# Retention and two feed-forward layers on one core: the lead of the displaced weight slots goes from 16 to 8 elements

## The chip, the cores and the metric

The kernel runs on one core of a Trainium2 chip. The metric is the device time of one execution in microseconds, the median of several runs.

## The reference

Attention with a decay instead of a softmax (retention), over 4 batches, 8 heads, 576 positions and 64 channels, gives 2304 tokens of 512 channels. Two feed-forward layers of 512 x 2048 x 512 follow, with different activations:

```python
ret = scores * Dmat[None, :, :, :]          # scores = scale * q k^T, Dmat = gamma**(i-j), lower triangle
attn_out = np.matmul(ret, v)                # -> x [2304, 512]
...
h = x @ w_in;  g = np.maximum(0.01 * h, h);  x = g @ w_out        # first layer
...
h = x @ w_in;  g = h - np.tanh(h);           out = g @ w_out      # second layer
```

## The kernel before

**Number format.** In the layers every operand is split into a high and a low part (fp32r), and every product is made of three matmuls: high by high, high by low, low by high. A matmul has a weight load of 128 x 128 of its own (128 columns of 4 bytes are 512 bytes in each partition) and then moves 512 or 256 columns (2048 or 1024 bytes in each partition).

**Stages.** `retention()` computes the retention chunk by chunk in fp32. Between its pieces it places 12 units of the first layer: `unit_h` (L782) multiplies 256 tokens by two blocks of `w_in` (matmuls of L789, 24 in a unit), `unit_o` (L802) multiplies the result by `w_out` (L814, 24 in a unit). All of these move 256 columns. `layers()` then goes through the list `steps`: a step is one block of 128 hidden channels by 512 or 256 tokens.

- First layer (`m == 0`): `h_mm` (L275) moves the activations `xh` and `xl`; `o_mm` (L428) moves the hidden activations `g`, with `w_out` as weights. 2304 tokens are blocks of 512 and a remainder of 256; in the first group some more of 256 went to the units of the retention stage.
- Second layer (`m == 1`): blocks of 512 tokens are "folded": one level of a Strassen-like scheme, in `h_folded` (L309), moves 256 columns of `xh`, `xl` or of the prepared combinations `xe`. `o_mm` (L428) moves 512 columns of `w_out`, with `g` as weights. In one folded pair of steps, pieces of L309 (6 to 18 matmuls) and of L428 (6 matmuls) alternate. The remainder of 256 tokens goes through `h_mm` with 256 columns.

The order of the work is written out by hand; no scheduler changes it.

**Addresses.** `xh`, `xl` and the store `w` of all weight and `g` slots lie one behind the other in one pool, and their sizes are multiples of 512 bytes. `xe` stands at the other end of the memory, behind a pad of 320 bytes. In the built program `xh`, `xl`, `xe` and `w` all begin at 160 bytes modulo 512. A slot in `w` is 4096 bytes, and a slot that is asked for with `lead` begins `LEAD` elements further on:

```python
    def slot(k, lead):                                              # L81
        at = k * 1024 + (LEAD if lead else 0)
    def w_place(m, g, j):                                           # L85
        return slot(N_OUT + N_G + (4 + j if m == 0 else j), m or g == 0)
    def w_out_place(m): ...  return slot((turn["o"] - 1) % N_OUT, m)       # L90
    def g_place(m): ...      return slot(N_OUT + (turn["g"] - 1) % N_G, m) # L94
    def g_at(s):                                                    # L343
        at = LEAD if m == 0 and n < 512 else 0
```

So the lead applies to `w_in` of the first group of the first layer and of the whole second layer, to `w_out` and `g` of the second layer, to `g` of the first layer where 256 columns move, and to `g` of the units in the retention stage. With `LEAD = 16` the distance "start of the moving operand minus start of the weights", modulo 512 bytes (called the gap below), is:

| matmuls | columns | count | gap |
|---|---|---|---|
| L309, second layer | 256 | 1344 | 448 (that is -64) |
| L275, second layer and first group of the first | 256 | 240 | 448 |
| L789, units | 256 | 288 | 448 |
| L814, units | 256 | 288 | 64 |
| L428, first layer | 256 | 192 | 64 |
| L275, first layer, first group | 512 | 48 | 448 |
| L275, first layer, other groups | 256 | 144 | 0 |
| L275, first layer, other groups | 512 | 576 | 0 |
| L428, first layer | 512 | 624 | 0 |
| L428, second layer (both operands with lead) | 512 | 864 | 0 |

Of the kernel before, what the change touches and what calls it, by code (L numbers as in the profile page):

```python
# [20 lines left out]

LEAD = 16

TANH_T = 0.5
RHO_C = 0.0020447001866573740
# [8 lines left out]
def retention_moe_moe(  # L36
# [41 lines left out]
    N_OUT, N_G, N_IN = GF, 3, 8  # L78
    wide_all = keep.tile([P, (N_OUT + N_G + N_IN) * 1024 + LEAD], F32R, name="w")

    def slot(k, lead):  # L81
        at = k * 1024 + (LEAD if lead else 0)
        return wide_all[:, at:at + 1024].rearrange("p (i c) -> p i c", i=2)
# [259 lines left out]
    def g_at(s):  # L343
        m, g, t0, n, f = steps[s]
        at = LEAD if m == 0 and n < 512 else 0
        return slice(at, at + n)
# [810 lines left out]
```

## Time and profile before

| | |
|---|---|
| median of 3 runs | 859.57 us (859.44 to 859.59) |
| the profiled execution | 860.67 us |
| its span, first to last instruction | 858.6 us |
| TensorE matmuls, busy | 844.0 us (98%) |
| TensorE weight loads, busy | 748.7 us (87%) |
| VectorE, ScalarE, GpSimd, busy | 605.7, 446.0, 376.0 us |

The profiled execution's own time is 2.07 us over its span and 1.10 us over the median. Matmuls are pipelined: the duration that a row gives to one is longer than the distance from its start to the start of the next. What a matmul costs in a row of equal ones is therefore read from starts: the start of the first row behind them, less their own start, divided by their count.

### The profile page before, as it was taken

To read this page: it belongs to the slowest core of one execution; us is meant where nothing else is said; L and a number is where in the kernel's file an instruction comes from. 1 tells how busy PE (TensorE), PEld (TensorE's weight loads), DVE (VectorE), ACT (ScalarE), POOL (GpSimd) and SP (SyncE) were. 2 spreads that over 40 slices of the span, in tenths; PEclk is the share of its full clock that TensorE was granted. 3 is DMA by queue.
4 is the path that set the end of the run, shared out by engine and by line. 5 is a ranking of instruction groups with operands and counts; after the bars stand their busy time and mean duration, and the time that the engine had idled before them with its cause. 6 is when DMAs were issued, how large, how long until landed. Compare 5 with 4: busy or idle time off the path is not lost.

```text
span 858.6 us, 15267 instructions
## 1 busy us (share of the span) xinstructions
PE 844.0 (98%) x5750; PEld 748.7 (87%) x5750; DVE 605.7 (71%) x1050; ACT 446.0 (52%) x877; POOL 376.0 (44%) x304
## 2 busy tenths in 40 slices
PE   6999999999999999999999999999999999999997
PEld 5899999888988888888888899888999899999996
DVE  5996876687685777658764687756766677677765
ACT  3553444453345334453544577765566566566663
POOL 2542231140046203364365387745445445544553
PEclk9999999999999999999999999999999999999999
DMA  9945754323455433645454512491225311563112
GB/s 326 327 134 182 232 191 168 127 100 131 138 199 211 155 122 101 243 172 150 169 188 155 196 56 94 158 357 73 75 98 203 141 74 74 207 234 123 50 50 74
DMA packets 38793, 134.42 MB, mean 157 GB/s; under 512 B 4416, under 2 KB 5952, under 8 KB 36672
## 3 DMA queue, kind: packets, MB, share of 16 engines
q1 hardware_dynamic: 38288, 133.25, 43.6%
q8 instruction: 45, 0.74, 0.3%
q10 hardware_dynamic: 432, 0.20, 0.1%
q14 instruction: 28, 0.23, 0.1%
HBM read 97.26 MB, written 36.18 MB: 155 GB/s over the span
## 4 chain that ended last, share of the span: by engine, by line
PE 92%; DVE 5%; issue 1%; DMA 1%; ACT 0%; POOL 0%; SPq 0%; DVEq 0%
PE a L428 41%; PE h L275 22%; PE h L309 18%; PE a L814 3%; PE x_b L789 3%; PE o L739 1%; PE sc L647 1%; PE o L728 1%; DVE cw L183 1%; DVE pt L670 1%; PE x_c L696 1%; DMA kv<-in_vn 1%; DVE xl L748 0%; DVE st L706 0%; DVE cw L172 0%
## 5 line engine op out<-in xcount | busy, mean ns | idle before, releaser
L428 PE MATMUL a<-w 128*128 128x512 f32 (+1 forms) x1680 | 394.3, 377 | 0.0
L428 PEld LDWEIGHTS a<-w 128*128 128x128 f32 x1680 | 293.4, 188 | 47.5
L256 POOL TENSOR_TENSOR w<-cw,w 128x512 fp32r<-128x512 f32 x80 | 113.4, 1433 | 230.8 <-ACT w L255 211.6
L275 PE MATMUL h<-xh,w 128*128 128x512 f32 (+1 forms) x672 | 187.0, 349 | 0.0
L368 POOL TENSOR_TENSOR v<-t,u 128x512 f32<-128x512 f32 (+1 forms) x76 | 93.5, 1230 | 97.8 <-ACT t L365 93.7
L275 PEld LDWEIGHTS h<-xh,w 128*128 128x128 f32 x672 | 119.4, 188 | 17.0
L400 POOL TENSOR_TENSOR w<-v,w 128x512 fp32r<-128x512 f32 (+1 forms) x76 | 95.9, 1262 | 62.9 <-ACT w L399 62.9
L354 ACT ACTIVATE w<-h 128x512 fp32r<-128x512 f32 (+1 forms) x68 | 37.2, 547 | 159.7 <-PE h L275 115.5
L275 PE MATMUL h<-xl,w 128*128 128x512 f32 (+1 forms) x336 | 117.0, 348 | 0.0
L309 PE MATMUL h<-xh,w 128*128 128x256 f32 x512 | 100.9, 281 | 0.1
L309 PEld LDWEIGHTS h<-xe,w 128*128 128x128 f32 x576 | 80.9, 189 | 9.5 <-DVE mk L303 1.8
L183 DVE SCALAR_TENSOR_TENSOR cw<-st,cw 128x512 uint32<-128x512 uint32 x96 | 86.5, 901 | 2.5
L394 DVE SCALAR_TENSOR_TENSOR v<-q,v 128x512 f32<-128x512 f32 (+1 forms) x76 | 61.9, 814 | 36.0 <-POOL v L368 36.0
L309 PEld LDWEIGHTS h<-xh,w 128*128 128x128 f32 x512 | 83.1, 190 | 2.7 <-DVE v L397 1.4
L309 PE MATMUL h<-xe,w 128*128 128x256 f32 x576 | 84.1, 282 | 0.4 <-DVE mk L303 0.4
L513 DVE TENSOR_TENSOR acc<-a,acc 128x512 f32<-128x512 f32 (+1 forms) x113 | 71.3, 657 | 17.0 <-PE a L428 17.0
L364 ACT ACTIVATE u<-h 128x512 f32<-128x512 f32 (+1 forms) x80 | 44.2, 553 | 73.3 <-DVE h L303 51.5
L399 ACT ACTIVATE w<-v 128x512 fp32r<-128x512 f32 (+1 forms) x76 | 45.3, 596 | 62.6 <-DVE v L397 60.1
L172 DVE TENSOR_SCALAR cw<-cw 128x512 f32<-128x512 f32 x64 | 35.1, 548 | 57.6 <-ACT cw L166 57.3
L309 PE MATMUL h<-xl,w 128*128 128x256 f32 x256 | 71.8, 281 | 0.0
L275 PEld LDWEIGHTS h<-xl,w 128*128 128x128 f32 x336 | 63.3, 188 | 8.6
L383 DVE TENSOR_TENSOR h<-h,t 128x512 f32<-128x512 f32 (+1 forms) x80 | 51.4, 642 | 14.8 <-ACT t L365 14.7
(89 smaller groups left out, 1161.7 us busy)
## 6 DMA issues: line engine op xcount, KB each, us to landing
kept<-w SPq DMA_DIRECT2D x48, 512.0 KB, 3.2
w<-kept SPq DMA_DIRECT2D x48, 512.0 KB, 4.8
xe<-xkept SPq DMA_DIRECT2D x12, 1536.0 KB, 6.4
st<-in_w2i SPq DMA_DIRECT2D x16, 512.0 KB, 3.5
st<-in_w1i SPq DMA_DIRECT2D x12, 512.0 KB, 4.3
st<-in_w1o SPq DMA_DIRECT2D x12, 512.0 KB, 3.5
xkept<-xe SPq DMA_DIRECT2D x4, 1536.0 KB, 10.5
kv<-in_vn SPq DMA_DIRECT2D x16, 320.0 KB, 4.9
```

The lines of the kernel that those rows point to most:

```text
L183: nc.vector.scalar_tensor_tensor(out=t["w"], in0=t[src], scalar=scalar, in1=t["w"], op0=op, op1=ALU.bitwise_or)
L256: nc.gpsimd.tensor_tensor(out=wp[:, 1, :], in0=wf, in1=wp[:, 0, :].bitcast(F32), op=ALU.subtract)
L275: nc.tensor.matmul(out=ps[:, :n], lhsT=w[:, wi, cs], rhs=x[:, kk, t0:t0 + n], start=kk == 0 and i == 0, stop=kk == KK - 1 and i == 2,)
L309: nc.tensor.matmul(out=out_, lhsT=w[:, wi_, at:at + P], rhs=x(xi, kk), start=start and kk == 0 and j == 0, stop=stop and kk == 1 and j == ...
L364: nc.scalar.activation(out=u[:, :n], in_=h, func=AF.Square)
L368: nc.gpsimd.tensor_tensor(out=v[:, :n], in0=t_[:, :n], in1=u[:, :n], op=ALU.mult)
L383: nc.vector.tensor_tensor(out=h, in0=h, in1=tmp[s][1][:, :n], op=ALU.subtract)
L394: nc.vector.scalar_tensor_tensor(out=v, in0=q, scalar=RHO_A, in1=v, op0=ALU.add, op1=ALU.mult)
L399: nc.scalar.activation(out=gt[:, 0, g_at(s)], in_=v, func=AF.Copy)
L400: (nc.gpsimd if m else nc.vector).tensor_tensor(out=gt[:, 1, g_at(s)], in0=v, in1=gt[:, 0, g_at(s)].bitcast(F32), op=ALU.subtract)
L428: nc.tensor.matmul(out=o, lhsT=l, rhs=r, start=f == 0 and i == 0 and d % pack == 0, stop=f == GF - 1 and i == 2 and (d + 1) % pack == 0, s ...
L513: nc.vector.tensor_tensor(out=dst, in0=a, in1=dst, op=ALU.add)
```

## The change

One constant becomes 8. Leads of 64 bytes become leads of 32 bytes: a gap of 448 becomes 480 (that is -32), a gap of 64 becomes 32, and a gap of 0 stays, since there both operands move or neither does. `w` gets 32 bytes shorter, so what is placed behind it (the tiles of the retention stage, two tiles of the second layer's activation) moves by 32 bytes as well. No instruction is added, removed or moved on any engine.

```diff
-LEAD = 16
+LEAD = 8
```

## Rows read from the trace of the kernel before

**Rows 1.** The page: span, busy time and share of TensorE, clock, chain by engine
```profile
span 858.6 us, 15267 instructions
PE 844.0 (98%) x5750; PEld 748.7 (87%) x5750; DVE 605.7 (71%) x1050; ACT 446.0 (52%) x877; POOL 376.0 (44%) x304
PEclk9999999999999999999999999999999999999999
PE 92%; DVE 5%; issue 1%; DMA 1%; ACT 0%; POOL 0%; SPq 0%; DVEq 0%
```

**Rows 2.** Busy time by stretch: retention, first layer, second layer
```profile
core 0: us, PE busy (x) PEld busy (x) DVE busy (x) ACT busy (x) POOL busy (x), PEclk, DMA share, GB/s
0.00:144.00 144.00, 134.64 (x1705) 125.79 (x1706) 111.49 (x239) 64.97 (x150) 47.66 (x52) 1.00 0.66 222
144.00:469.00 325.00, 325.00 (x1623) 276.45 (x1622) 226.69 (x368) 142.86 (x277) 115.41 (x82) 1.00 0.46 160
469.00:858.60 389.60, 384.35 (x2426) 346.49 (x2424) 267.54 (x443) 238.21 (x451) 212.95 (x172) 1.00 0.35 130
```

**Rows 3.** Groups by line and shape, TensorE: count, busy us, mean ns, idle before
```profile
L309 PE MATMUL h<-xh,w 128*128 128x256 f32 x512 | 100.9, 281 | 0.1
L309 PE MATMUL h<-xe,w 128*128 128x256 f32 x576 | 84.1, 282 | 0.4 <-DVE mk L303 0.4
L309 PE MATMUL h<-xl,w 128*128 128x256 f32 x256 | 71.8, 281 | 0.0
...
L428 PE MATMUL a<-w 128*128 128x256 f32 x192 | 25.2, 280 | 0.0
```

**Rows 4.** Timeline, TensorE, second layer: start, us, line, operands, count
```profile
662.17 2.88 PE L428 MATMUL a<-w 128*128 128x512 f32 x12
664.89 0.28 PE L275 MATMUL h<-xh,w 128*128 128x256 f32 x1
...
666.30 2.88 PE L428 MATMUL a<-w 128*128 128x512 f32 x12
669.02 0.28 PE L275 MATMUL h<-xh,w 128*128 128x256 f32 x1
```

**Rows 5.** Timeline, TensorE, first layer, gap 0 with 256 columns
```profile
217.50 0.40 PE L275 MATMUL h<-xh,w 128*128 128x256 f32 x2
217.74 0.28 PE L275 MATMUL h<-xl,w 128*128 128x256 f32 x1
217.85 0.40 PE L275 MATMUL h<-xh,w 128*128 128x256 f32 x2
218.09 0.28 PE L275 MATMUL h<-xl,w 128*128 128x256 f32 x1
218.22 0.28 PE L275 MATMUL h<-xh,w 128*128 128x256 f32 x1
218.34 2.91 PE L428 MATMUL a<-w 128*128 128x512 f32 x12
221.08 0.28 PE L275 MATMUL h<-xh,w 128*128 128x256 f32 x1
...
222.51 2.91 PE L428 MATMUL a<-w 128*128 128x512 f32 x12
225.26 0.28 PE L275 MATMUL h<-xh,w 128*128 128x256 f32 x1
```

**Rows 6.** Chain of waits, longest pieces in order of time: start, us, line, count
```profile
145.73 4.09 PE h L275 x36
...
154.02 2.80 PE h L275 x12
...
231.13 2.76 PE h L275 x12
...
477.70 2.83 PE h L275 x24
```

**Rows 7.** Chain of waits, pieces in order of time, one unit in the retention stage
```profile
81.91 2.72 PE a L814 x24
...
88.47 2.94 PE x_b L789 x24
```

**Rows 8.** Timeline, TensorE, second layer, at two short waits of TensorE
```profile
487.32 0.97 PE L309 MATMUL h<-xe,w 128*128 128x256 f32 x6
488.13 0.86 PE L428 MATMUL a<-w 128*128 128x512 f32 x3
488.83 0.96 PE L309 MATMUL h<-xe,w 128*128 128x256 f32 x6
```

**Rows 9.** Timeline, TensorE, first layer, first group: where the quicker spacing ends
```profile
149.66 1.53 PE L428 MATMUL a<-w 128*128 128x256 f32 x12
151.02 0.28 PE L275 MATMUL h<-xh,w 128*128 128x256 f32 x1
...
152.44 1.58 PE L428 MATMUL a<-w 128*128 128x256 f32 x12
```

## The prediction

> **What bounds the kernel now.** I read the page first. TensorE is busy for 98% of the span and makes 92% of the chain of waits, and its clock was granted in full in every slice [rows 1]. The stretches say the same with more detail: from 144 us on TensorE idles only 5.25 us in all, and 9.4 us in the retention stage before, while VectorE, the next busiest engine, works 605.7 of 858.6 us [rows 1, 2]. So the time is the number of matmuls times their spacing, and a nanosecond more or less per matmul arrives at the end almost undiminished. Durations do not tell the spacing: they are 281 or 282 ns for 256 columns in all groups [rows 3]. I therefore took starts from the timeline and lengths of unbroken pieces from the chain, and put beside each the gap that the code gives (moving operand minus weights, modulo 512 bytes).
>
> **What the gap does today.** With 512 columns and a gap of 0, twelve matmuls take 662.17 to 664.89, or 226.7 ns each [rows 4]; with a gap of 448 twelve take 2.80 us, or 233.3 ns [rows 6]. With 256 columns and a gap of 0, seven take 217.50 to 218.34, or 120.0 ns each [rows 5]; with a gap of 448 in the second layer 24 take 2.83 us, or 117.9 ns [rows 6]. The same gap of 448 has a second, quicker spacing: 36 matmuls at 145.73 take 4.09 us, or 113.6 ns [rows 6], and 24 of L814 at a gap of 64 take 2.72 us, or 113.3 ns [rows 7]. At 151.02 the quick spacing ends: twelve of L428 before it go at 113.3 ns, and twelve of L275 behind it, at the old gap, at 118.3 ns [rows 9]. So a spacing depends on the gap and also on how the stream was entered. Lastly the way out counts. Twelve matmuls of 512 columns behind a block at gap 448 take 666.30 to 669.02, 2.72 us, as anywhere [rows 4]. Behind a block at gap 0 they take 2.74 and 2.75 us [rows 5], some 25 ns more, and behind one at gap 64 they take 2.76 us [rows 6], 40 ns more. Today's gap thus has a way out that costs nothing, and it is taken 142 times in the second layer (I counted the places on the timeline where a row of L428 with 512 columns stands behind one of L309 or L275).
>
> **The change part by part.** Nothing is added, removed or reordered; only spacings can move. No trace shows a gap of 480 or of 32 in these matmuls, so each term is bounded by the nearest gaps, 0 on one side and 448 or 64 on the other. 480 lies in the middle between 448 and 512, which is 0, and 32 between 0 and 64, and I take the middle of the prices too.
>
> Term A, 256 columns in the two layers: 512 + 576 + 256 = 1344 of L309 [rows 3], 240 of L275 (48 in the first group, 192 in the second layer, by the code) and 192 of L428 [rows 3], together 1776. From 117.9 ns to the middle between 117.9 and 120.0, which is 118.95: +1.05 x 1776 = +1.9 us. Bounds: 120.0 ns gives +2.1 x 1776 = +3.7 us; the quick 113.3 ns gives -4.6 x 1776 = -8.2 us.
>
> Term B, the 142 ways out into 512 columns: from 0 to the middle between 0 and 25 ns, +12.5 x 142 = +1.8 us. Bounds: 0, and 40 ns, which is +5.7 us. Less than nothing is not to be had there, since 2.72 us is what twelve such matmuls take with no disturbance.
>
> Term C, 288 + 288 matmuls of the units in the retention stage, which are at 113.3 ns now [rows 7] (of L789 the 24 from 88.47 take 2.94 us with a wait at their head): the middle between 113.3 and 120.0 is 116.7, +3.35 x 576 = +1.9 us. Bounds: 0, if the quick spacing survives, and +6.7 x 576 = +3.9 us. TensorE is the chain there as well, so this isn't hidden.
>
> Term D, 48 matmuls of 512 columns in the first group: from 233.3 to the middle, 230.0: -3.3 x 48 = -0.2 us, between -0.3 and 0.
>
> Term E, what moves without a change of its gap: 864 matmuls of L428 in the second layer, whose two operands both move by 32 bytes. Those of the first layer, without the lead, and these, 64 bytes further on, have one spacing today, 226.7 ns ([rows 4] for these; the rows of twelve in [rows 5] differ by the way out alone). A move by 64 bytes does nothing, then; one by 32 isn't shown. I take 0 and keep one step between spacings that occur, 233.3 - 226.7 = 6.6 ns, as a bound either way: 5.7 us. The fp32 matmuls of the retention stage, whose tiles move by 32 bytes together, and the operands of VectorE, ScalarE and GpSimd I take at 0: those three have 253 us or more of slack over the span [rows 1]. If that cover were gone, the 5.25 us of idle time in the second layer [rows 2] is where it would show first.
>
> Sum: +1.9 + 1.8 + 1.9 - 0.2 = **+5.4 us**. For the profiled execution, 860.67 us (span 858.6 and 2.07 around it), that is 866.1 us; it stood 1.10 us over the median, so for the median it is 859.57 + 5.4 = **865.0 us**, 0.6% more.
>
> **A rule that speaks against any change.** The rows say that 512 columns cost 226.7 or 233.3 ns with nothing but the place of the weights being different [rows 4, 6]. The Trainium skill, page "TensorE: Matmul & The Clock Gate", section "Step-by-step: what each phase is for", states that the moving operand and the weight load have independent read ports, and that loading the next weights takes no read bandwidth from the running matmul. By that rule every term above is 0 and the time stays at 859.6 us. This trace disagrees with it by those 6.6 ns, so I give it a rival's place, not the forecast.
>
> **The rivals.**
>
> 1. *Like a gap of 0.* 32 bytes may be too little to part the two streams. Then all upper ends hold, with 25 ns for the way out: 3.7 + 3.6 + 3.9 - 0.3 = +10.9 us, 870.5 us. For it: the price at 0 and at 448 differs by only 2.1 ns, so the useful distance may be the whole 64 bytes. Against it: nothing shows a threshold.
>
> 2. *Faster: the quick spacing holds in the second layer.* The 113.3 ns exist at gaps of 448 and 64, so the weights can keep up. The mechanism is the entry: behind 512 columns the stream falls at once into 117.9 ns, and only behind a wait of TensorE does it get quick. If at 480 it enters at 113.3 ns, term A is -8.2 us, and with ways out between 0 and 25 ns (0 to +3.6 us) the time is 851.4 to 855.0, say 853 us. Three matmuls of 512 columns behind such a quick stretch, 488.13 to 488.83, took 0.70 us instead of 0.68 [rows 8], so the way out is probably not free. It decides itself where the average of a block of 12 falls below 117.9 - 25/12 = 115.8 ns; above that, a free way out lost costs more than the spacing gives. Term E at its favourable end would be added.
>
> 3. *No change.* Either the two streams meet in units of 64 bytes or more, so that 32 and 64 bytes count alike, or the retention gap and the layers' gap shift against each other to near nothing: 859.6 us, within 1.7.
>
> **How the numbers follow.** This kernel's measurement can tell about 0.2%, 1.7 us, from no change. The forecast, something between the neighbours, has 0.34 (861.5 to 868 us); rival 1 has 0.14 (868 to 872); rival 2 has 0.32 (851 to 857.8), since an unknown place in a system with two spacings may as well land in the better one; rival 3 has 0.20. Slower is 0.34 + 0.14 = 0.48, the same 0.20, faster 0.32. The range goes from 852 to 871: it holds the forecast, most of rival 1 and 2, and leaves out what term E might add at either end. The likeliest case's own range is 861.5 to 868.
>
> **What would show it.** In the trace of the changed kernel: the spacing of 12 matmuls of L275 between two blocks of L428 in the second layer (now 118; forecast 119, rival 1: 120, rival 2: 113); the twelve of L428 behind them (now 2.72 us; 2.73 forecast, 2.75 by rival 1); 24 of L814 (now 2.72 us; 2.80 forecast, 2.88 by rival 1); and 512 columns in the second layer away from a way out (226.7 ns, if term E is nothing). The forecast is wrong if the 256-column blocks get quicker than 117.9 ns, or if a spacing changes whose gap did not.

## The result, and the profile after

The changed kernel takes **865.18 us** (863.40 to 865.46) beside 859.58 us for the kernel before on the same chip: 5.6 us more between the medians. The ratio, which compares means, is 1.0056 (1.0042 to 1.0069), or 4.8 us. Forecast were 865.0 us, 5.4 us slower. The profiled execution took 865.04 us instead of 860.67, and its span grew by 4.4 us; the accounting below divides up that span.

The page of the changed kernel, the lines that answer to [rows 1]:

```profile
span 863.0 us, 15267 instructions
PE 849.1 (98%) x5750; PEld 752.2 (87%) x5750; DVE 604.5 (70%) x1050; ACT 446.0 (52%) x877; POOL 374.9 (43%) x304
PE 95%; DVE 2%; issue 1%; DMA 1%; POOL 0%; ACT 0%; SPq 0%; DVEq 0%; POOLq 0%
```

The same instructions, the same 98%, and a chain that is TensorE's even more than before. The three stretches of the changed kernel answer to [rows 2]:

```profile
core 0: us, PE busy (x) PEld busy (x) DVE busy (x) ACT busy (x) POOL busy (x), PEclk, DMA share, GB/s
0.00:144.00 144.00, 135.20 (x1694) 126.35 (x1694) 110.75 (x239) 64.09 (x148) 46.54 (x51) 1.00 0.66 221
144.00:469.00 325.00, 325.00 (x1631) 276.88 (x1628) 226.35 (x368) 142.42 (x276) 114.51 (x81) 1.00 0.46 160
469.00:863.00 394.00, 388.93 (x2432) 348.93 (x2431) 267.41 (x445) 239.52 (x454) 213.81 (x172) 1.00 0.35 129
```

The clock is granted in full in all three. TensorE idles 5.07 us in the last stretch (5.25 before), so the added time isn't waiting: TensorE's matmuls stand further apart. In the first 144 us it starts 1694 matmuls where it started 1705; it is behind already when the retention stage ends.

The longest pieces of the chain of waits of the changed kernel (start, us, what) answer to [rows 6, 7]:

```profile
88.92 3.04 PE x_b L789 x24
91.96 2.80 PE a L814 x24
...
147.21 4.26 PE h L275 x36
...
232.74 2.75 PE h L275 x12
...
479.20 2.84 PE h L275 x24
```

24 of L814 went from 2.72 to 2.80 us (116.7 ns each), 36 of L275 in the first group from 4.09 to 4.26 (118.3 ns, where the quicker spacing of 113.6 had been), 24 of L275 in the second layer from 2.83 to 2.84. The way out is read on the timeline of the changed kernel, TensorE, which answers to [rows 4]:

```profile
665.01 2.91 PE L428 MATMUL a<-w 128*128 128x512 f32 x12
667.75 0.28 PE L275 MATMUL h<-xh,w 128*128 128x256 f32 x1
...
669.17 2.91 PE L428 MATMUL a<-w 128*128 128x512 f32 x12
671.92 0.28 PE L275 MATMUL h<-xh,w 128*128 128x256 f32 x1
```

665.01 to 667.75 is 2.74 us and 669.17 to 671.92 is 2.75 us for twelve matmuls of 512 columns, where [rows 4] had 2.72; the twelve of 256 columns between them, 667.75 to 669.17, take 1.42 us, 118.3 ns each.

For the whole kernel I took the distance from each matmul's start to the next start in both traces and summed the differences by group:

| matmuls | gap | change, us | term and forecast |
|---|---|---|---|
| 1344 of L309 | -64 to -32 | +1.04 | A |
| 192 of L275, second layer | -64 to -32 | +0.09 | A |
| 48 of L275, 256 columns, first group | -64 to -32 | +0.16 | A |
| 192 of L428, 256 columns | 64 to 32 | -0.09 | A: together +1.20, forecast +1.9 |
| 888 of L428, 512 columns, behind blocks of the second layer | 0, the way out from -64 to -32 | +1.82 | B: forecast +1.8 |
| 288 of L789 and 288 of L814 | -64 to -32, 64 to 32 | +1.13 and +0.66 | C: +1.79, forecast +1.9 |
| 48 of L275, 512 columns, first group | -64 to -32 | +0.01 | D: forecast -0.2 |
| first layer, gap unchanged | 0 | -0.12 in all | E: forecast 0 |
| fp32 matmuls of the retention | unchanged | -0.45 | E: forecast 0 |

The 888 are the 864 of the second layer and two blocks of twelve of the first, which run between blocks of L275 of the second. The sum is +4.25 us; with a first matmul that starts 0.14 us later that is the span's +4.4.

### The profile page after: what moved, and what is told of

Read it like the earlier page. It is cut to its first block, busy times and chain, and to the rows that moved or that the text cites. A ratio compares the mean times of both kernels' runs of the same rounds, so it can differ in the third digit from the quotient of the medians.

```text
span 863.0 us, 15267 instructions
## 1 busy us (share of the span) xinstructions
PE 849.1 (98%) x5750; PEld 752.2 (87%) x5750; DVE 604.5 (70%) x1050; ACT 446.0 (52%) x877; POOL 374.9 (43%) x304
## 4 chain that ended last, share of the span: by engine, by line
PE 95%; DVE 2%; issue 1%; DMA 1%; POOL 0%; ACT 0%; SPq 0%; DVEq 0%; POOLq 0%
PE a L428 41%; PE h L275 22%; PE h L309 18%; PE a L814 4%; PE x_b L789 4%; PE o L739 2%; PE sc L647 2%; PE o L728 1%; PE x_c L696 1%; DMA kv<-in_vn 1%; PE x_e L660 0%; POOL w L256 0%; DVE cw L183 0%; PE x_e L654 0%; DVE v L394 0%
## 5 line engine op out<-in xcount | busy, mean ns | idle before, releaser
L428 PE MATMUL a<-w 128*128 128x512 f32 (+1 forms) x1680 | 396.3, 378 | 0.0
L428 PEld LDWEIGHTS a<-w 128*128 128x128 f32 x1680 | 293.5, 188 | 49.3
L275 PE MATMUL h<-xh,w 128*128 128x512 f32 (+1 forms) x672 | 187.1, 349 | 0.0
L275 PEld LDWEIGHTS h<-xh,w 128*128 128x128 f32 x672 | 119.5, 188 | 16.9
L275 PE MATMUL h<-xl,w 128*128 128x512 f32 (+1 forms) x336 | 117.3, 349 | 0.0
L309 PE MATMUL h<-xh,w 128*128 128x256 f32 x512 | 101.7, 282 | 0.0
L309 PEld LDWEIGHTS h<-xe,w 128*128 128x128 f32 x576 | 81.0, 188 | 9.4 <-DVE mk L303 1.5
L309 PEld LDWEIGHTS h<-xh,w 128*128 128x128 f32 x512 | 82.9, 188 | 2.6 <-DVE v L397 1.3
L309 PE MATMUL h<-xe,w 128*128 128x256 f32 x576 | 84.3, 282 | 0.3 <-DVE mk L303 0.3
L309 PE MATMUL h<-xl,w 128*128 128x256 f32 x256 | 71.9, 281 | 0.0
L275 PEld LDWEIGHTS h<-xl,w 128*128 128x128 f32 x336 | 63.3, 188 | 8.6
```

The lines of the kernel that those rows point to most:

```text
L275: nc.tensor.matmul(out=ps[:, :n], lhsT=w[:, wi, cs], rhs=x[:, kk, t0:t0 + n], start=kk == 0 and i == 0, stop=kk == KK - 1 and i == 2,)
L309: nc.tensor.matmul(out=out_, lhsT=w[:, wi_, at:at + P], rhs=x(xi, kk), start=start and kk == 0 and j == 0, stop=stop and kk == 1 and j == ...
L428: nc.tensor.matmul(out=o, lhsT=l, rhs=r, start=f == 0 and i == 0 and d % pack == 0, stop=f == GF - 1 and i == 2 and (d + 1) % pack == 0, s ...
```

## Experiments

Each run is timed beside the kernel before on the same chip; "gap" is again moving operand minus weights. "Way out" is the time that a run of 512 columns behind 256 columns takes over 226.7 ns for each of its matmuls, in the median. A "seam" is the place where the number of columns changes; its gap is the last moving operand before it minus the first weights behind it. Sums "by starts" come from the one execution of each run whose trace is kept, "L428 with 512 columns" being the 888 above.

**Does the place count, or the distance?** All operands 32 bytes further on, all gaps as before (lines move by one).

```diff
-        [P, 80], F32, name="edge"
+        [P, 72], F32, name="edge"
+    keep.tile([P, 8], F32, name="pad")
```

> The lead stays at 16, so every gap is as before; all operands (xh, xl, xe, w and the tiles behind them) stand 32 bytes further on, as the displaced slots and the tiles behind w do (in the other direction) in the change. Gap theory (the distance of moving operand and weights sets the spacing): nothing moves, 859.6 us within 0.2%; 117.9 ns for 256 columns and 226.7 ns for 512 in the second layer, no price for the way out. Place theory (the address itself, modulo 64 bytes, sets it): the spacings of the changed kernel or others, 863 us or more, or a gain.

Measured: 860.72 beside 860.80 us, ratio 0.9999 (0.9990 to 1.0009). The chain of waits of this run:

```profile
91.89 2.72 PE a L815 x24
...
661.51 1.41 PE h L276 x12
662.93 2.72 PE a L429 x12
```

2.72, 1.41 and 2.72 us are the figures of the kernel before. A place 32 bytes further on is worth nothing by itself; what is left of the change is the distance.

**The two halves of the change, each alone.** The new lead in the second layer only, and in the units and the first layer only. For both, `slot` takes a number in place of a flag:

```diff
+LEAD_IN, LEAD_OUT = 8, 8
...
-        at = k * 1024 + (LEAD if lead else 0)
+        at = k * 1024 + lead
...
-        return slot(N_OUT + N_G + (4 + j if m == 0 else j), m or g == 0)
+        return slot(N_OUT + N_G + (4 + j if m == 0 else j), LEAD_IN if m else LEAD * (g == 0))
...
-        return slot((turn["o"] - 1) % N_OUT, m)
+        return slot((turn["o"] - 1) % N_OUT, LEAD_OUT * m)
...
-        return slot(N_OUT + (turn["g"] - 1) % N_G, m)
+        return slot(N_OUT + (turn["g"] - 1) % N_G, LEAD_OUT * m)
```

> Lead 8 in the second layer alone (w_in, w_out and g of it), 16 elsewhere. Gap theory: what the two traces differ by in the second layer, L309 +1.0, L275 +0.1, the way out +1.8, together +2.9 us: 862.5 us; 118.3 ns for 256 columns and some 15 ns for each way out. If the second layer's part came from what runs before it (another phase of the stream on entry), nothing: 859.6 us.

Measured: 864.03 us, ratio 1.0038 (1.0026 to 1.0050), +3.2 us. By starts, L309 +1.05 us, L275 +0.10, L428 with 512 columns +1.83; the units unchanged.

The other half has `LEAD = 8` and `LEAD_IN, LEAD_OUT = 16, 16`.

> Lead 8 in the units of the retention stage and in the first layer, 16 in the second layer. w keeps its size, so the tiles of the retention stage stay where they were. Gap theory: L789 +1.1, L814 +0.7, first group +0.2, together +1.9 us: 861.5 us, the fp32 matmuls as before. If the 32 bytes by which the retention tiles moved made that stage's difference: 859.6 us. The parts of this run and of the run with lead 8 in the second layer alone should add up to the whole change.

Measured: 862.29 us, ratio 1.0017 (1.0007 to 1.0026), +1.5 us. By starts, L789 +1.06 us, L814 +0.74, the 48 of L275 with 256 columns +0.17, those with 512 columns 0.00. The second layer keeps its old spacing: the chain of waits of this run shows a unit at 2.80 us and the later block at 2.72.

```profile
90.94 2.80 PE a L815 x24
...
666.97 2.72 PE a L429 x12
```

3.2 and 1.5 us make 4.7 of the 5.6, and the ratios 0.55 of 0.56%; by starts the halves add up to the whole (2.98 + 1.97 beside 4.90 us for the same groups). The two halves don't visibly act on each other.

**No lead, twice the lead, four times the lead.** One constant each: `LEAD = 0`, `LEAD = 32`, `LEAD = 64`.

> Lead 0: every gap is 0. By the rows of before at a gap of 0 (120.0 ns for 256 columns, 25 ns for each way out into 512 columns, 226.7 ns for 512): 1776 x 2.1 = +3.7, 142 x 25 ns = +3.6, 576 x 6.7 = +3.9, the 48 of 512 columns -0.3, together +10.9 us: 870.5 us. If the middle price of the changed kernel is no step between two ends but the price of every small gap: 865 us.

Measured: 869.51 us beside 860.80, ratio 1.0101 (1.0086 to 1.0115), +8.7 us. The chain of waits:

```profile
93.25 2.88 PE a L814 x24
...
663.03 1.44 PE h L275 x12
```

> Lead 32, a gap of 384 (-128) and 128. If the price falls steadily with the distance (120.0 at 0, 118.3 at 32, 117.8 at 64 bytes): 117.5 ns or a little less in the layers, at most -0.5 us, and a way out of unknown price between 0 and 40 ns, up to +5.7 us. If the quick 113.3 ns is what a stream gets that starts far enough from a meeting: -8.0 us before the way out. If both streams meet in any case once in a weight load, whatever the distance: the layers as before, 859.6 us.

Measured: 871.11 us beside 859.28, ratio 1.0134 (1.0118 to 1.0149), +11.8 us: the dearest of all and beyond every figure that was expected, although its two streams are further apart. The chain of waits:

```profile
92.44 2.84 PE a L814 x24
...
663.00 1.44 PE h L275 x12
```

> Lead 64, a gap of 256 in all displaced matmuls, half of the 512 bytes, as far as two streams can be apart. The same three theories as with lead 32: a steady fall, at most -0.5 us before the way out (0 to +5.7 us); the quick spacing, -8.0 us before the way out; no difference, 859.6 us.

Measured: 868.07 us, ratio 1.0103 (1.0084 to 1.0122), +8.8 us. The chain of waits:

```profile
91.37 2.88 PE a L814 x24
...
661.15 1.44 PE h L275 x12
```

A distance of 256 bytes costs what a distance of 0 costs: L309 takes 161.25 us in both kernels, L428 with 512 columns 205.57 and 205.58. So the price repeats after **256 bytes**, not 512, and the gap of 448 in the prediction is -64, that of 480 is -32. The five leads side by side (changes against the kernel before, by starts except for the time; the spacing is the median of the unbroken blocks of 256 columns in the second layer):

| lead | gap of 256 columns | time, us | L309, us | its spacing, ns | way out, ns | L428 with 512, us | units, us |
|---|---|---|---|---|---|---|---|
| 0 | 0 | +8.7 | +2.24 | 119.3 | 27 | +2.98 | +2.96 |
| 8 | -32 | +5.6 | +1.04 | 118.3 | 15 | +1.82 | +1.79 |
| 16 | -64 | 0 | 0 | 117.8 | 0 | 0 | 0 |
| 32 | -128 | +11.8 | +2.84 | 119.8 | 41 | +4.46 | +2.42 |
| 64 | -256 | +8.8 | +2.25 | 119.3 | 27 | +2.98 | as lead 0 |

The 576 matmuls of L275 whose gap stays at 0 serve as a control: with the four other leads their sum moves by less than 0.1 us. Lead 32 has its 256 columns at -128, where 512 columns of L275 cost 232 ns (11.14 us for the 48 of the first group).

**What the way out is made of.** The lead of `w_in` at 16 and of `w_out` and `g` at 8: 256 columns keep -64 and 512 columns keep 0, but at both seams, into 512 columns and back, the operand that still moves stands -32 from the first weights of the next block.

```diff
+LEAD_IN, LEAD_OUT = 16, 8
```

> The other half: in the second layer w_out and g have the lead of 8, w_in keeps 16. The 864 matmuls of 512 columns keep their gap of 0 and move by 32 bytes (term E alone); the 256-column ones stay at 448. Gap theory: 226.7 ns and 117.8 ns as before, 0 for term E; at the seam g loads at a gap of 480. If the way out's price is left behind by the 256-column stream: 0, no change at all. If the gap at the seam makes it: +1.8 us. If the place counts: 226.7 ns becomes 220 or 233 ns, 5.7 us either way.

Measured: 863.17 us beside 859.28, ratio 1.0041 (1.0026 to 1.0056), +3.9 us, more than the 1.8 expected of a seam. L428 with 512 columns costs 4.10 us more, though its own gap is what it was, and L309 1.05 us less. The timeline, TensorE:

```profile
667.46 2.94 PE L429 MATMUL a<-w 128*128 128x512 f32 x12
670.24 0.28 PE L276 MATMUL h<-xh,w 128*128 128x256 f32 x1
```

2.78 us for twelve, 231.7 ns each. So the distance at the seams counts, and it can set the pace of all that follows. By position in the runs of six, before: 227, 227, 227, 227, 227, 232 ns; with the change: 233, 233, 227, 228, 228, 231; here: 231, 235, 231, 234, 228, 238. With the change the first two matmuls pay and the stream finds back; here it doesn't.

The counterpart, `w_in` at 8 and the others at 16, **missed its aim**:

```diff
+LEAD_IN, LEAD_OUT = 8, 16
```

> In the second layer w_in alone has the lead of 8, w_out and g keep 16. The 256-column matmuls run at a gap of 480, the 512-column ones at 0, but at the seam the weights that load under the last 256 columns (g) stand at a gap of 448 to them. If the way out's price is left behind by the 256-column stream: 118.3 ns and some 15 ns for each way out, +2.9 us over before, as with both at 8. If it is the gap at the seam that makes it: 118.3 ns and 0, +1.2 us.

Measured: 900.28 us, ratio 1.0473 (1.0458 to 1.0489). The last `g` slot with a lead of 16 reaches 8 elements into the first `w_in` slot with a lead of 8, so that each overwrites a piece of the other, the second layer computes something else, and the two wait for each other. The waits of TensorE (us in total, times, longest us):

```profile
PE h L310 <- POOL w L401: 18.7, 4, 5.2
...
PE h L276 <- POOL w L401: 4.5, 1, 4.5
```

These waits are new; of the spacing the run says nothing.

**More distances in one run.** Each group of the second layer with a `w_in` lead of its own, and 64 elements of room between the slots:

```diff
+IN_LEADS = (8, 24, 48, 56)
+G_LEAD, OUT_LEAD = 16, 16
```

> In the second layer w_in stands at another lead in each of its four groups: 32, 96, 192 and 224 bytes (gaps of -32, -96, +64 and +32 modulo 256); w_out and g keep 64 bytes, units and first layer keep 64. Each slot of w_in has 256 bytes of room behind it, so that no two slots overlap; half of the slots thereby change their distance from 0 to 256 or from 448 to 192 modulo 512. If the price repeats every 256 bytes: units and first layer as before (117.3 to 118.5 ns in the units, 119.3 and 226.7 ns in the first layer). Group 0 asks the seam question again, stream at -32, weights of g at -64 to it: 118.3 ns in both cases; a way out of 15 ns if the stream leaves it behind, 0 if the seam makes it. For the others: a spacing of 117 to 120 ns by the prices seen so far; the quick 113.3 ns is what would beat both kernels, 1.7 us in each group.

Measured, one execution of each: 864.58 us beside 861.36. Group times are read from starts in the traces, from the first L309 of a group to that of the next (the last one to the same matmul of its last block of L275). The four groups have gaps of -32, -96, +64 and +32 and took 96.41, 95.61, 80.29 and 94.56 us, where before they took 95.37, 94.68, 79.53 and 93.72: each about 1 us more. The way out is 26, 26, 27 and 32 ns, although the seam towards 512 columns is at -64 as before; what changed is the distance of the 256 columns themselves and the seam back, and the run doesn't separate the two. The first group repeats the question of the run with overlapping slots and answers neither 0 nor 15 ns but some 26. Half of the `w_in` slots of the units and the first layer went from a distance of 0 to 256, or from -64 (448) to -64 (192), with no change over 0.15 us: the period again.

In the next, 512 columns are at +64:

```diff
+IN_LEADS = (16, 24, 48, 56)
+G_LEAD, OUT_LEAD = 16, 32
```

> In the second layer w_out at 128 bytes and g at 64, so that the 512-column matmuls run at a gap of +64 instead of 0; w_in at 64, 96, 192 and 224 bytes in groups 0 to 3. If the price of 512 columns has its least value at 0 (233.3 at -64, 232 at -128): 230 ns and more, some 3 us or more over before from 864 matmuls. If the side matters (moving operand ahead of the weights, as at +64 with 256 columns, where 116.9 to 118.1 ns were seen): 220 to 226 ns, up to 5.7 us less than before. Group 0 against before shows what the seams then cost.

Measured, one execution of each: 861.76 us beside 861.36. The third group, with 256 columns at +64, keeps the quick spacing from 689 us to its end at 751, as its chain of waits shows:

```profile
699.72 2.04 PE h L312 x18
701.76 1.39 PE a L431 x6
```

2.04 us is 113.3 ns each; but six of 512 columns take 1.39 us, 231.7 ns. The group takes 79.25 us, 0.28 less than before: what the one block gains the other gives back.

The last scan has everything at +64, +32, -32 and -64 with `w_out` at 256 bytes:

```diff
+IN_LEADS = (48, 56, 72, 80)
+G_LEAD, OUT_LEAD = 48, 64
```

> Second layer with w_out at 256 bytes (0 modulo 256) and g at 192, so 512 columns run at +64; w_in at 192, 224, 288 and 320 bytes in groups 0 to 3, which gives 256-column gaps of +64, +32, -32 and -64; the weights of g stand at +64 to the last 256 columns everywhere. The run before had its quick spacing, 113.5 ns, where all of 256 at +64, 512 at +64 met, but 512 columns then cost 5 ns more each. If a seam whose gap equals that of the stream is free, as at -64 in the kernel before: group 0 gives 113.5 ns and no way out, at least 1.7 us less than before in that group (93.7 us of 95.4). If the way out is the price of having been quick: 113.5 ns and 30 ns per way out, and the group is within 0.5 us of before. Groups 1 to 3 have unequal seams: 116.9 to 118.5 ns and ways out of 25 to 35 ns.

Measured, one execution of each: 860.43 us beside 859.36. The groups take 95.32, 95.52, 80.36 and 92.98 us. The first one, the best hope, is where it was (95.37); the last one is 0.74 us quicker than before (93.72). Its chain of waits, from its beginning:

```profile
751.43 2.09 PE h L312 x18
...
761.77 2.05 PE h L312 x18
763.82 1.37 PE a L431 x6
```

2.05 us for 18 is 113.9 ns, with 1.37 us for six of 512 columns, 228.3 ns: quick 256 columns, and 512 columns only 1.6 ns over their 226.7.

**The candidate.** The distances of that last group in all four:

```diff
+IN_LEAD, G_LEAD = 80, 48
...
-        return slot((turn["o"] - 1) % N_OUT, m)
+        return slot((turn["o"] - 1) % N_OUT, 0)
```

> The last group of the run before, everywhere in the second layer: w_in at 64 bytes (modulo 256), g at 192, w_out at 0, so that 256 columns run at a gap of -64, 512 columns at +64, and the weights of g stand at +64 to the last 256 columns. That group took 92.98 us where the kernel before takes 93.72. If the gaps alone set the price, also in the other groups: 114.4 ns for 256 columns, 15 ns for a way out, and -0.74 x 4 = -3.0 us, 856.6 us. If it was the phase in which the stream arrived in that one group: 859.6 us or more, with 117.8 ns again.

Measured: 863.26 us (861.79 to 864.35) beside 859.70, ratio 1.0035 (1.0022 to 1.0047): slower, where 856.6 was expected. The groups take 95.23, 95.58, 80.83 and 95.38 us. With the same addresses the stream has **two paces**. The chain of waits, where one turns into the other:

```profile
603.64 2.05 PE h L310 x18
605.69 1.37 PE a L429 x6
...
611.88 0.75 PE h L310 x6
612.63 1.40 PE a L429 x6
614.03 2.13 PE h L310 x18
616.16 1.40 PE a L429 x6
617.56 1.42 PE h L310 x12
```

Until 611.88 it is 2.05 us for 18 and 1.37 for six; from there 2.13 (118.3 ns) and 1.40 (233.3 ns), and apart from some 4 us at 678 it stays so to the end. The change falls on a piece of six that takes 0.75 us instead of 0.69. The timeline of the weight loads has a short wait there:

```profile
611.65 0.77 PEld L310 LDWEIGHTS h<-xe,w 128*128 128x128 f32 x6 [0.21 <-DVE mk L304]
```

A weight load waited 0.21 us for VectorE, and the stream that went in quick came out slow. It goes the other way too. The timeline of TensorE, some 25 us earlier, at another such place:

```profile
584.57 0.28 PE L310 MATMUL h<-xh,w 128*128 128x256 f32 x1
...
585.99 0.85 PE L429 MATMUL a<-w 128*128 128x512 f32 x3
...
587.09 0.28 PE L310 MATMUL h<-xl,w 128*128 128x256 f32 x1
...
588.35 0.85 PE L429 MATMUL a<-w 128*128 128x512 f32 x3
```

584.57 to 585.99 are twelve at 118.3 ns; behind a wait of 0.2 us before 586.87, eleven from 587.09 to 588.35 go at 114.5. From the first L309 on, 13 weight loads of this trace waited longer than 0.1 us, all for VectorE, and no other longer than 0.06. The pace changes eight times, each time directly behind or inside one of these waits, the shortest of which (0.13 us at 516.59, too short for the views to list) stands before the change at 517 us; behind the other five the pace stays. That waits tip the pace at these addresses is thus what the trace suggests. They are not all that can do it: in the scan with `OUT_LEAD = 32` the quick spacing sets in at 689.22, and the last such wait there is at 682.83. No run took a wait away to test it, and why a wait tips the pace one way, the other way or not at all stays open.

No kernel here is measurably quicker than the one before.

## Why the prediction was right, and where it wasn't

- **What bounds the kernel** held: TensorE's spacing, and a nanosecond per matmul arrives at the end. The other engines' busy times are what they were [rows 1] and no wait in the layers is new. (One reading was loose: [rows 3] has 280 ns beside 281 and 282, which changes nothing.)
- **Term B** (the way out) was the largest in the trace and right: +1.82 us for a forecast of +1.8. Its middle, 12.5 ns, compares with 15 in the median and 1.82 / 142 = 12.8 in the mean. It is a mean that was right: the three blocks of twelve from 660 to 672 us have 15, 27 and 28 ns, so that the place that the prediction named, twelve of L428 behind L275, showed rival 1's 2.75 us rather than the 2.73 of the forecast.
- **Term C** was right: +1.79 us for +1.9, L814 at the forecast 116.7 ns.
- **Term A** had the right sign and was too large by 0.7 us. Its 1344 of L309 cost 1.04 us more, 0.77 ns each, where the step "from 117.9 ns to the middle between 117.9 and 120.0" gave 1.05. The middle was right, its upper neighbour wasn't: a gap of 0 in the second layer adds 2.24 us / 1344 = 1.67 ns, not the 2.1 that the first layer's 120.0 ns suggested [rows 5]. The 192 of L428 (117.8 ns in the mean before, 117.3 after) had no part in it, where the forecast had given them 0.2 us.
- **Term D** was nothing instead of -0.2 us: at -32 the 48 matmuls take what they take at -64.
- **Term E** held for the place (ratio 0.9999). 512 columns away from a way out stayed at 227 ns in the median. The term had nothing for the fp32 matmuls of the retention, -0.45 us: their three longest distances from start to start came to 3.60 us instead of 4.17. That is no effect of the change that could be told from chance, for the same sum stands between +0.35 and -1.81 us in the traces of the other leads and scans, and at -0.57 where only the second layer was changed.
- **From the profiled execution to the median.** For the profiled execution the sum gave 866.1 us and it took 865.04; A (0.7 too much) and the fp32 waits are most of that miss, and D takes back 0.2. The median came out nearer, 865.18 for 865.0, because the execution profiled after stands 0.14 us under its median, where the one before stood 1.10 over. So 5.4 against 5.6 us flatters the terms; by starts it is 5.4 against 4.25, and between the means 4.8. That the median fell so close to the forecast is luck.
- **The mean of two neighbours** held near home: at -32 L309 has 0.77 ns of 1.67, the way out 15 ns of 27, the units 1.79 us of 2.96. But the picture behind it, that a greater distance parts the streams better, falls with the lead of 32: at -128, the furthest apart that a period of 256 bytes allows, the kernel loses 11.8 us. The mean of two neighbours is thus a rule that came out here, not one that the runs explain. The period of 512 bytes, by which I wrote the gaps, was an assumption that no row of the kernel before could show.
- **Rival 1** (like a gap of 0) is measured by the lead of 0: 8.7 us rather than the 10.9 computed, and the change isn't that.
- **Rival 2** (the quick spacing holds) isn't what happens at -32: behind the same waits of TensorE as in [rows 8], no block of the second layer gets under 117 ns. The quick spacing can hold at other distances, as the scans show, and there the objection about the way out decides as the prediction put it: in the group at +64 the blocks of 512 columns gave back all but 0.28 us.
- **Rival 3** (no change) falls, and with it, for this kernel, what I had drawn from a rule. The Trainium skill, page "TensorE: Matmul & The Clock Gate", section "Step-by-step: what each phase is for", has the weight load take no read bandwidth from the running matmul. Here five leads with the same instructions in the same order differ by up to 11.8 us, while moving all operands together does nothing. The runs don't show by which path the one operand disturbs the other, nor whether the engines that write the moved slots have a part in it.

## What to carry to other kernels

Where TensorE is the chain, read spacings from starts, not from durations, and write beside each the distance between moving operand and weights modulo 256 bytes; here that alone is worth 1.3% between the best and the worst of one constant (ratio 1.0134). Judge a distance by the whole sequence, with the places where the shape changes, since a block of 256 columns that gains 4 ns per matmul can cost the block of 512 behind it as much. And run a candidate that was found in one group over the whole kernel before believing it: here 0.74 us gained in one group became 3.6 us lost in four.

## What the hardware showed that was not expected

- The price of a distance repeats after 256 bytes: distances of 0 and 256 give the same sums to 0.01 us in the second layer (161.25 us for 1344 matmuls), and half of the slots that L789 reads could go from 448 to 192 for 0.1 us. Other pairs were not compared.
- It isn't monotone: 119.3, 118.3, 117.8 and 119.8 ns at 0, -32, -64 and -128, with 27, 15, 0 and 41 ns for the way out.
- 512 columns at an unchanged distance of 0 go at 226.7 or 231.7 ns, depending on the distance at the seam between two blocks.
- One and the same set of addresses has two paces, 114 and 228 to 229 ns, or 118 and 233 ns, for 256 and 512 columns. Either held over tens of microseconds at a granted clock of 1.00. Why, of all the distances run here, only those of the kernel before have a way out that is free nearly everywhere (under 4 ns in 119 of 141 places) stays open; distances that are no multiple of 32 bytes were not tried.
